# Strided q and k of the first batch: whole 256-byte rows and TensorE transposes in place of half rows and VectorE transposes

## The chip, the cores and the metric

The kernel runs on one core of one Trainium2 chip. The metric is the device time of one execution in microseconds (us); lower is better. The inputs and outputs lie in the chip's memory (HBM), and the kernel is one launch.

## The reference

Three layers, chained. First, attention with 4 batches, 8 heads, 576 tokens and 64 numbers a head. Heads 0 to 3 look at a local window of 32 keys, heads 4 to 7 at the keys of the same residue modulo 32:

```python
rel = pos[:, None] - pos[None, :]
mask_local = (rel >= 0) & (rel < 32)
mask_strided = (rel >= 0) & (pos[None, :] % 32 == pos[:, None] % 32)
scores = np.where(mask, q @ k.T / 8, -1e9)
attn = softmax(scores)                       # + 1e-9 in the denominator
x = (attn @ v) laid out as 2304 tokens x 512
x = (x @ w_a) * (x @ w_b) @ w_out            # 512 -> 1536 -> 512
h = x @ w_in2
out = (h / (1 + exp(-h))) @ w_out2           # 512 -> 2048 -> 512
```

The weights come as 64-bit floats. The kernel rebuilds 32-bit floats from their two halves, and splits each operand into a high and a low part so that three passes of TensorE give the wanted precision.

## The kernel before

The instructions of every engine are written out by hand, in order. Each engine (PE is TensorE, DVE VectorE, ACT ScalarE, POOL GpSimd, SP SyncE's DMA queue) works its own list strictly in that order, and an instruction waits until its inputs are there and its output's place is free.

The start-up, some 55 us, computes the attention of batch 0 alone. It is a loop over stages s from -1 to 16. Units 0 to 4 are the local heads (128 tokens each), units 5 to 8 the strided heads (eight or nine residues each). In stage s the kernel takes scores of unit s, the softmax of unit s-1, the turn (transpose of the probabilities) of unit s-3 and the product with v and the store of unit s-5. Inside a stage the order is the string `ORDER = "AXPV0QWS1LGRTBKUON2Y"`, of which these letters matter here:

- A: at s = 11, 12, 15 and 16 (`PART`) the first half of one up projection of the next layer, into the accumulators acc0 to acc3 in this order (`up(partial[i], ...)`, L683).
- P: TensorE transposes of the local q and k (`turn_pair`, L296) and their copies out of PSUM (L307, L309).
- V and O: the product with v (L540) and the store of x: two copies by ACT (L568), then two subtractions by DVE (L571), all from the PSUM tile of V.
- Q: at s = 2, 3 and 4 (`TQ`) the transposes of the strided q and k (`transpose_qk`, L275).
- S, L, X: the scores (mask L414, product L417), their maximum (L452), the exponential (L466).
- R: at s = 3, 5 and 7 `prepare` copies the strided q of a unit together (L385); it reads all of the transposed q.
- T and U: the turn (L500) and its copy out (L512, L518).
- K: `keep_warm`, products of ones into a bank that nobody reads (L773); `WARM1` says how many in which stage, seven at s = 3.
- 0, B, 1, 2, Y: the conversion of one 64-bit weight piece (L642, L629, L650, L655) and its split (L675, L676), at the stages in `CONV`.

In the first batch every PSUM tile of attention comes from `att_tile`, which deals seven tiles in turn: two "ring", two "att" and acc0, acc1, acc2. The tile that a request gets depends only on how many were asked for before. From s = 15 on it deals four, without the accumulators.

The loads of the start-up are a written list too (`LOADS[-2]`), worked off by SP's queue, a few by ACT's (capital letters). In it t4 and t5 take the strided q and k of batch 0 (`load_qk(1)`, L264): eight transfers, each of 32 partitions x 36 pieces of 128 bytes (half a row of 64 floats), in the layout that DVE's 32x32 block transposes want. Behind them in SP's queue stand the loads of v (L321, L330, L353), weight pieces (L603, L605), and batch 1's q and k (L264 again, the same two buffers).

After the start-up come the blocks of the up and down projections, some 2.7 us of TensorE each, into which the attention of batches 1 to 3 and the conversion of the other weights are planned. The start of the blocks is the end of the start-up; nothing later has a fixed time.

Of the kernel before, what the change touches and what calls it, by code (L numbers as in the profile page):

```python
# [9 lines left out]
F32 = mybir.dt.float32  # L10
# [8 lines left out]
P = 128  # L19
# [14 lines left out]

PREP = {-1: (0, 1, 2, 3, 4), 3: (5, 6), 5: (7,), 7: (8,)}
PAIR = {-1: 0, 0: 1, 2: 2}
TQ = {2: (0,), 3: (1,), 4: (2, 3)}

LOADS = {
    -2: (  # L40
        "q0 Q1 i M1 K2 S1 w0 V1 k0 k1 s1 t4 t5 v0 M7 r8 s1 s1 s1 w2 s2 s1 S1 w1 s1 s1 s1 w4 "
        "w3 s4 Q2 u2 u5 u2"
    ),
    -1: "b",
# [67 lines left out]
def attention_gated_mlp_silu_mlp(  # L112
# [15 lines left out]
    nc = tc.nc  # L128
    B, H, S, D = q.shape
# [32 lines left out]
    lpool = att_ctx.enter_context(tc.tile_pool(name="lpool", bufs=1, side="right"))  # L162
    qpool = att_ctx.enter_context(tc.tile_pool(name="qpool", bufs=2, side="right"))
    apool = att_ctx.enter_context(tc.tile_pool(name="apool", bufs=3, side="right"))

    ident = cpool.tile([P, P], F32, name="ident")
# [11 lines left out]
    def acc_tile(i):  # L178
        return accp.tile([P, 512], F32, tag=f"acc{i}", name=f"acc{i}")

    def ring_tile():
        return ringp.tile([P, 512], F32, tag="ring", name="ring")

    att_turn = [0]
    feed = [nc.sync]

    def att_tile(wide):
        n = att_turn[0]
        att_turn[0] += 1
        if wide:  # L190
            n %= wide
            if n < 2:
                return ring_tile()
            if n >= 4:
                return acc_tile(n - 4)
        return attp.tile([P, 512], F32, tag="att", name="att")
# [19 lines left out]
    def x_tile(g):  # L216
        if g == NG - 1 and g not in x_t:
            both["s"] = t = home(1)
            x_t[g] = two(t[:, :4])
        if g not in x_t:  # L220
            x_t[g] = xpool.tile([P, 2, CC, G], F32R, tag="x%d" % HOMES["x"][g], name="x")
        return x_t[g]
# [10 lines left out]
    class Batch:  # L233
# [38 lines left out]
        def transpose_qk(self, ty, one=None):  # L272
            for i in range(4) if one is None else (one,):
                t, o, c = self.loaded[i // 2], self.T[ty][i // 2], i % 2
                nc.vector.transpose(out=o[:, c], in_=t[:, c].rearrange("p j i -> p (j i)"))  # L275

        def load_pair(self, m, i):

            if not self.T:
                self.T[0] = [qpool.tile([P, 2, S], F32, tag=nm, name=nm) for nm in ("qT", "kT")]  # L280
                self.pairs = {}
            p0, n = PAIRS[m]
            self.pairs[m, i] = t = rpool.tile([P, 4, 2 * D], F32, tag="raw", name="pair")
            feed[0].dma_start(
                out=t[:n],
                in_=(q, k)[i][self.b, 0:4, 2 * p0:2 * (p0 + n), :].rearrange("h (p s) d -> p h (s d)", s=2),
            )
# [345 lines left out]
    def merge_w(c, step, early=False):  # L633
        if c is None or (c < EARLY and not early):
            return
        pair = words[c].rearrange("p (n two) -> p n two", two=2)
        low, high = pair[:, :, 0], pair[:, :, 1]
        if step == 0:
            made[c] = rpool.tile([P, DM], F32, tag="raw", name="raw")
            z = made[c].bitcast(I32)  # L640
            if early:
                nc.vector.tensor_single_scalar(out=z, in_=low, scalar=29, op=ALU.logical_shift_right)  # L642
            else:


                top = words[c].bitcast(U8).rearrange("p (n eight) -> p n eight", eight=8)[:, :, 3]
                nc.scalar.activation(out=z, in_=top, func=AF.Copy, scale=1.0 / 32, bias=-31.0 / 64)  # L647
        elif step == 1:
            z = made[c].bitcast(I32)
            nc.vector.scalar_tensor_tensor(  # L650
                out=z, in0=high, scalar=SIGN, in1=z, op0=ALU.bitwise_and, op1=ALU.bitwise_or
            )
        else:
            z = made[c].bitcast(I32)
            nc.vector.scalar_tensor_tensor(  # L655
                out=z, in0=rebased.pop(c), scalar=3, in1=z, op0=ALU.logical_shift_left, op1=ALU.bitwise_or
            )
            del words[c]
            if c < NA:
                raw[c] = made[c]  # L660
# [19 lines left out]
    def up(ps, w, x, T, chunks=range(CC)):  # L680
        for c in chunks:
            for wi, xi in PASSES:
                nc.tensor.matmul(  # L683
                    ps[:, :T],
                    lhsT=w[:, wi, c * P:(c + 1) * P],
                    rhs=x[:, xi, c, :T],
                    start=(c == 0 and wi == 0 and xi == 0),
                    stop=(c == CC - 1 and wi == 1),
                )
# [73 lines left out]
    with tc.manual_schedule():  # L763
# [6 lines left out]
        def keep_warm(n):  # L770

            for _ in range(n):
                nc.tensor.matmul(idle, lhsT=still, rhs=nc.const_aps.tensor(1.0, [P, 512], BF16), start=True, stop=True)  # L773

        batch = Batch(0, 7)
        nu = len(batch.units)
        every = lambda loads: [None for _ in loads]
        after = Batch(1, False)
        qs0, vs0, q1 = batch.load_qk(1), batch.load_vs(), after.load_qk(0)
        vl0 = batch.load_vl()  # L780

        masks = [epool.tile(list(t.shape), F32, tag="e", name="mask") for t in (mask_loc, mask_str)]
# [32 lines left out]
        for s in range(-1, max(nu + LV, max(PART), max(CONV) + 1) + 1):  # L815
            def stage(f, d):
                if 0 <= s - d < nu:
                    f(s - d)

            if s >= TAIL:  # L820
                batch.wide = 4
            now, last = CONV.get(s), CONV.get(s - 1)
            for step in ORDER:
                if step == "P" and s in PAIR:
                    for i in range(2):
                        batch.turn_pair(PAIR[s], i)
                        batch.turned_pair(PAIR[s], i)
                elif step in "SVTXLGNOU":
                    f, d = {
                        "S": (batch.scores, 0), "L": (batch.largest, 0), "X": (batch.softmax, 1),  # L830
                        "G": (batch.guard, 1), "N": (batch.normalise, 1), "T": (batch.turn, LT),
                        "U": (batch.turned, LT), "V": (batch.values, LV), "O": (batch.store, LV),
                    }[step]
                    stage(f, d)
                elif step == "K":
                    keep_warm(WARM1.get(s, 0))
                elif step == "A" and s in PART:
                    i = PART[s]
                    partial[i] = acc_tile(i)
                    up(partial[i], split[i], x_tile(0), G, (0, 1))  # L840
                elif step == "Q":
                    for i in TQ.get(s, ()):
                        batch.transpose_qk(1, i)
                elif step == "R":
                    for u in PREP.get(s, ()):
                        batch.prepare(u)
                elif step in "012" and now is not None:
                    merge_w(now, int(step), True)
                elif step == "B" and now is not None:
                    rebase_w(now, True)  # L850
                elif step == "Y" and last is not None and last < EARLY:
                    keep_w(last)
                    split_w(last)
                elif step == "W":
                    startup_loads(LOADS.get(s, ""))
        batch = after
# [356 lines left out]
        for m, key in enumerate(in_order):  # L1213
            t = ready[key]
            if m >= 4:
                t = max(t, held[in_order[m - 4]][1])
# [5 lines left out]
        for m, key in enumerate(in_order):  # L1222
            t = used[key][0] - LEAD_SPLIT
            t = max(t, used[in_order[m - 5]][1] if m >= 5 else (m - 5) * BLOCK)
# [34 lines left out]
        for key in in_order:  # L1259
            t = splits[key]  # L1260
# [3 lines left out]
            elif key[0] == "B":  # L1264
                n, c = key[1:]
                kind, j = ("ab"[c], n[1]) if n[0] == "o" else ("i", n[1] + c)
                needs((kind, j), (n, c, 0), t)
            elif key[0] == "B22":
                for c in range(2):
                    n = key[1]  # L1270
                    kind, j = ("ab"[c], n[1] + H1) if n[0] == "o" else ("i", n[1] + c + H2)
                    needs((kind, j), (n, c, 1), t)
            elif key[0] == "T12":
                n, c = key[1:]
# [21 lines left out]
        for m, key in enumerate(in_order):  # L1296
            lo, _, piece = need[key]
            t = lo - LEAD_RAW
            t = max(t, need[in_order[m - 10]][1] + 0.01 if m >= 10 else (m - 10) * BLOCK)
# [3 lines left out]
        p = 0  # L1303
        ys = {}
        for ph, g in PHASES:
# [7 lines left out]
            for kind, j in half[ph]:  # L1313
                if batch.b < B and p == PLAN[batch.b][0]:
                    batch = plan_attention(batch, *PLAN[batch.b])
                work = block(p)
                w = next(work)
                if kind in "abi":
                    rest = range(CC)
                    if p in partial:  # L1320
                        ps, rest = partial[p], (2, 3)
                    else:
                        ps = ring_tile()
# [9 lines left out]
                    else:  # L1333
# [4 lines left out]
                            out=g2, in0=th, scalar=1.0, in1=ps, op0=ALU.add, op1=ALU.mult  # L1338
                        )
                        acts[j] = split_act(g2, T)  # L1340
                elif kind == "o":
                    h = acts.pop(j)
# [9 lines left out]
                    if j == N1 - 1:  # L1352
                        ys[g] = y = xpool.tile([P, 2, CC, G], F32R, tag="x%d" % HOMES["y"][g], name="y")
                        for d in range(CC):
                            nc.scalar.copy(out=y[:, 0, d], in_=accs[d])
                            nc.vector.tensor_tensor(
                                out=y[:, 1, d], in0=accs[d], in1=y[:, 0, d].bitcast(F32), op=ALU.subtract
# [3 lines left out]
                else:  # L1361
                    h = acts.pop(j)
# [14 lines left out]
            for t in range(T // P):  # L1377
                pool, tag = ((epool, "e"), (epool, "e"), (tpool, "a"), (tpool, "h32"))[t]
# [48 lines left out]
```

## Time and profile before

| | us |
|---|---|
| three timed runs | 957.92, 956.31, 957.80 (median 957.80) |
| the profiled execution, its own time | 954.39 |
| its span in the trace | 952.6 |

| engine | busy us | share of the span |
|---|---|---|
| PE | 928.5 | 97% |
| DVE | 663.9 | 70% |
| ACT | 542.6 | 57% |
| POOL | 80.4 | 8% |

The span is the time from the first to the last instruction of the profiled execution; 1.8 us of its own time lie around it. Shares are means over the whole span. The change lies in the first 55 us, so the views below are of that stretch. The mean granted TensorE clock over the span is 0.988 of full speed.

### The profile page before, as it was taken

How to read it: one execution, taken by the hardware profiler on the slowest of the kernel's cores; microseconds unless marked ns; L12 is line 12 of the kernel's file. 1: busy time of each engine (PE TensorE's matmuls, PEld its weight loads, DVE VectorE, ACT ScalarE, POOL GpSimd, SP SyncE). 2: the span in 40 equal slices, each digit the busy share in tenths (PEclk: the TensorE clock that was granted, in tenths of full speed). 3: DMA queues.
4: the chain of work that ended last, by engine and by line, in shares of the span. 5: the costliest groups of instructions: out<-in, count | busy, mean ns of one | idle time of the engine just before them, and what ended most of it. 6: DMA issues, size and time to landing. Idle time of an engine off the chain costs nothing.

```text
span 952.6 us, 15861 instructions
## 1 busy us (share of the span) xinstructions
PE 928.5 (97%) x5626; PEld 749.6 (79%) x5626; DVE 663.9 (70%) x1248; ACT 542.6 (57%) x1274; POOL 80.4 (8%) x138
## 2 busy tenths in 40 slices
PE   9999999999999899999999999999999989999998
PEld 5767777787777677778888888888998768888897
DVE  4588888866767766666777666765587666765475
ACT  3558788566667665465544444345565555554364
POOL 2232222111111110100000000000000000000000
PEclk9799999999999999999999999999999999999999
DMA  9999899898698994322332222223464121234371
GB/s 165 198 271 269 248 254 271 248 294 240 224 267 208 264 223 133 105 86 89 100 105 83 67 67 67 57 83 112 126 185 125 44 67 56 78 107 148 108 212 47
DMA packets 163647, 145.29 MB, mean 153 GB/s; under 512 B 96800, under 2 KB 119904, under 8 KB 163568
## 3 DMA queue, kind: packets, MB, share of 16 engines
q1 hardware_dynamic: 154758, 121.81, 48.1%
q0 software_dynamic: 6720, 21.63, 6.8%
q10 hardware_dynamic: 2090, 0.84, 0.5%
q8 instruction: 44, 0.72, 0.3%
q14 instruction: 35, 0.29, 0.1%
HBM read 121.70 MB, written 22.54 MB: 151 GB/s over the span
## 4 chain that ended last, share of the span: by engine, by line
PE 75%; DVE 11%; ACT 8%; issue 3%; DMA 2%; SPq 0%; DVEq 0%; POOL 0%; ACTq 0%; POOLq 0%
PE ring L683 17%; PE ring L958 10%; PE att L958 8%; PE acc L1019 8%; PE acc L1365 7%; PE acc L1145 4%; PE att L1019 4%; PE ring L1019 4%; PE acc L1345 4%; PE acc L683 3%; ACT prs L466 2%; DVE w L676 2%; DVE raw L650 2%; PE att L540 1%; ACT raw L647 1%
## 5 line engine op out<-in xcount | busy, mean ns | idle before, releaser
L683 PE MATMUL ring<-x,w 128*128 128x512 f32 (+1 forms) x816 | 165.5, 356 | 1.5 <-DVE w L676 1.5
L683 PEld LDWEIGHTS ring<-x,w 128*128 128x128 f32 x816 | 132.4, 189 | 23.4 <-DVE w L676 2.0
L1241 DVE TENSOR_TENSOR w<-raw,w 128x512 fp32r<-128x512 f32 (+1 forms) x164 | 106.3, 656 | 30.3 <-ACT w L1240 27.5
L1240 ACT CAST w<-raw 128x512 fp32r<-128x512 f32 (+1 forms) x164 | 95.8, 593 | 18.6 <-PE att L1019 11.0
L676 DVE TENSOR_TENSOR w<-raw,w 128x512 fp32r<-128x512 f32 x136 | 92.8, 686 | 8.6 <-ACT w L675 7.9
L683 PE MATMUL ring<-y,w 128*128 128x512 f32 x384 | 96.1, 400 | 2.2 <-DVE g L1337 0.8
L1365 PE MATMUL acc<-w,h 128*128 128x512 f32 x384 | 93.9, 394 | 0.0
L683 PEld LDWEIGHTS ring<-y,w 128*128 128x128 f32 x384 | 71.9, 191 | 18.8 <-DVE w L676 1.1
L675 ACT CAST w<-raw 128x512 fp32r<-128x512 f32 x136 | 82.8, 619 | 4.0 <-DVE raw L655 3.9
L1365 PEld LDWEIGHTS acc<-w,h 128*128 128x128 f32 x384 | 70.9, 188 | 15.4
L693 ACT CAST h<-h 128x512 fp32r<-128x512 f32 (+1 forms) x48 | 27.3, 568 | 95.1 <-DVE h L1331 48.1
L1345 PE MATMUL acc<-h,w 128*128 128x512 f32 x288 | 70.8, 395 | 0.0
L958 PE MATMUL ring<-operands,w 128*128 128x512 f32 x240 | 61.4, 398 | 2.4 <-ACT w L1240 2.0
L694 DVE TENSOR_TENSOR h<-g,h 128x512 fp32r<-128x512 f32 (+1 forms) x64 | 39.9, 624 | 33.4 <-ACT h L693 33.2
L1345 PEld LDWEIGHTS acc<-h,w 128*128 128x128 f32 x288 | 53.0, 188 | 11.5
L693 ACT CAST h<-g 128x512 fp32r<-128x512 f32 (+1 forms) x64 | 36.3, 568 | 44.8 <-DVE g L1337 30.4
L958 PE MATMUL att<-operands,w 128*128 128x512 f32 x240 | 60.2, 395 | 0.0
L958 PE MATMUL ring<-x,w 128*128 128x512 f32 x240 | 59.2, 391 | 1.0 <-ACT u L969 1.0
L466 ACT ACTIVATE prs<-sm,nm 128x54 f32<-128x54 f32 (+1 forms) x120 | 39.8, 336 | 30.5 <-DVE nm L452 30.4
L958 PEld LDWEIGHTS ring<-operands,w 128*128 128x128 f32 x240 | 44.7, 188 | 14.8 <-ACT w L1240 2.7
L650 DVE SCALAR_TENSOR_TENSOR raw<-words,raw 128x512 int32<-128x512 int32 x68 | 47.6, 699 | 9.5 <-ACT raw L647 8.9
L958 PEld LDWEIGHTS ring<-x,w 128*128 128x128 f32 x240 | 44.9, 188 | 11.1 <-ACT u L969 1.4
(200 smaller groups left out, 1577.1 us busy)
## 6 DMA issues: line engine op xcount, KB each, us to landing
raw<-keptp SPq DMA_DIRECT2D x80, 256.0 KB
raw<-kepti SPq DMA_DIRECT2D x64, 256.0 KB
words<-in_moe_w_out_dram SPq DMA_DIRECT2D x28, 512.0 KB
raw<-kepto SPq DMA_DIRECT2D x48, 256.0 KB
raw<-kepta SPq DMA_DIRECT2D x36, 256.0 KB
raw<-keptb SPq DMA_DIRECT2D x36, 256.0 KB
words<-in_moe_w_in_dram SPq DMA_DIRECT2D x16, 512.0 KB
words<-in_moe_w_a_dram SPq DMA_DIRECT2D x12, 512.0 KB
```

Of the source, the lines that this page charges most:

```text
L466: nc.scalar.activation(out=place[s], in_=src[:, s], func=AF.Exp, bias=st["nm"][:, s:s + 1], scale=1.0, accum_out=su[:, s:s + 1],)
L650: nc.vector.scalar_tensor_tensor(out=z, in0=high, scalar=SIGN, in1=z, op0=ALU.bitwise_and, op1=ALU.bitwise_or)
L675: nc.scalar.copy(out=o[:, 0], in_=t)
L676: nc.vector.tensor_tensor(out=o[:, 1], in0=t, in1=o[:, 0].bitcast(F32), op=ALU.subtract)
L683: nc.tensor.matmul(ps[:, :T], lhsT=w[:, wi, c * P:(c + 1) * P], rhs=x[:, xi, c, :T], start=(c == 0 and wi == 0 and xi == 0), stop=(c == CC ...
L693: nc.scalar.copy(out=o[:, 0, :T], in_=t32[:, :T])
L958: nc.tensor.matmul(self.acc[acc], lhsT=w[:, wi, (2 * part + c) * P:(2 * part + c + 1) * P], rhs=x[:, xi, c], start=(begin and c == 0 and m ...
L1019: nc.tensor.matmul(accs[d], lhsT=lhsT, rhs=rhs, start=(first and wi == 0 and xi == 0), stop=(last and wi == 1))
L1240: nc.scalar.copy(out=o[:, 0, cols], in_=t)
L1241: nc.vector.tensor_tensor(out=o[:, 1, cols], in0=t, in1=o[:, 0, cols].bitcast(F32), op=ALU.subtract)
L1345: nc.tensor.matmul(accs[d], lhsT=w[:, wi, d * P:(d + 1) * P], rhs=h[:, xi], start=(j == 0 and wi == 0 and xi == 0), stop=(j == N1 - 1 and ...
L1365: nc.tensor.matmul(accs[t][:, :DM], lhsT=h[:, xi, t * P:(t + 1) * P], rhs=w[:, wi, :], start=(j == 0 and wi == 0 and xi == 0), stop=(j == ...
```

## The change

The strided q and k of batch 0 are loaded by `load_rows` instead of `load_qk`: for q and for k, four transfers (one a head) of 128 partitions x 4 rows of 256 bytes for the first 512 tokens, and two transfers of 64 partitions x 2 rows for the last 64. That is 12 transfers instead of 8, and 4608 pieces of 256 bytes instead of 9216 of 128. At step Q, `turn_rows` transposes them on TensorE into a PSUM tile from `att_tile` (four 128x128 transposes for i = 0 to 3, two of 64 tokens for i = 4 and 5) and `turned_rows` copies the tile out, i = 0 and 3 on ACT and the others on DVE. Batches 1 to 3 keep the old way.

```diff
-TQ = {2: (0,), 3: (1,), 4: (2, 3)}
+TQ = {2: (0,), 3: (1, 4), 4: (2, 3, 5)}
+TOKENS = 4
+ROWS_A = (0, 3)
-        "q0 Q1 i M1 K2 S1 w0 V1 k0 k1 s1 t4 t5 v0 M7 r8 s1 s1 s1 w2 s2 s1 S1 w1 s1 s1 s1 w4 "
+        "q0 Q1 i M1 K2 S1 w0 V1 k0 k1 s1 t6 t7 v0 M7 r8 s1 s1 s1 w2 s2 s1 S1 w1 s1 s1 s1 w4 "
+        def load_rows(self, ty):
+            tiles = [lpool.tile([P, TOKENS + 1, 4, D], F32, tag=nm, name=nm) for nm in ("qld", "kld")]
+            self.loaded = tiles
+            self.T[ty] = [qpool.tile([P, 2, S], F32, tag=nm, name=nm) for nm in ("qT", "kT")]
+            whole = P * TOKENS
+            for src, t in zip((q, k), tiles):
+                for h in range(4):
+                    hp, c = divmod(h, 2)
+                    feed[0].dma_start(
+                        out=t[:, :TOKENS, 2 * c + hp],
+                        in_=src[self.b, 4 * ty + h, :whole].rearrange("(n p) d -> p n d", p=P),
+                    )
+                    yield
+                for hp in range(2):
+                    h0 = 4 * ty + 2 * hp
+                    feed[0].dma_start(
+                        out=t[:S - whole, TOKENS, hp::2],
+                        in_=src[self.b, h0:h0 + 2, whole:].rearrange("c p d -> p c d"),
+                    )
+                    yield
+        def turn_rows(self, i):
+            self.turns = getattr(self, "turns", {})
+            self.turns[i] = ps = att_tile(self.wide)
+            if i < 4:
+                parts = [(self.loaded[i // 2][:, n, 2 * (i % 2):2 * (i % 2) + 2], P) for n in range(TOKENS)]
+            else:
+                n = S - P * TOKENS
+                parts = [(self.loaded[i - 4][:n, TOKENS, 2 * c:2 * c + 2], n) for c in range(2)]
+            for m, (t, n) in enumerate(parts):
+                nc.tensor.transpose(ps[:, m * n:(m + 1) * n], t.rearrange("p h d -> p (h d)"), ident[:n, :n])
+        def turned_rows(self, ty, i):
+            ps, o = self.turns.pop(i), self.T[ty][i // 2 if i < 4 else i - 4]
+            copy = nc.scalar.copy if i in ROWS_A else nc.vector.tensor_copy
+            if i < 4:
+                copy(out=o[:, i % 2, :P * TOKENS], in_=ps)
+            else:
+                n = S - P * TOKENS
+                copy(out=o[:, :, P * TOKENS:], in_=ps[:, :2 * n].rearrange("p (c t) -> p c t", c=2))
-        qs0, vs0, q1 = batch.load_qk(1), batch.load_vs(), after.load_qk(0)
+        qs0, vs0, q1 = batch.load_rows(1), batch.load_vs(), after.load_qk(0)
                 elif step == "Q":
                     for i in TQ.get(s, ()):
-                        batch.transpose_qk(1, i)
+                        batch.turn_rows(i)
+                        batch.turned_rows(1, i)
```

## Rows read from the trace of the kernel before

**Rows 1.** The chain of waits, 9 to 54 us: start, length, what held the end.

```profile
9.23 1.06 PE att L296 x8
...
16.42 0.29 PE att L296 x4
...
20.93 0.37 PE att L500 x2
...
47.73 1.40 PE acc L683 x6
...
52.57 0.55 PE acc L773 x2
53.14 0.56 DVE x L571 x2
```

**Rows 2.** Who waited, 9 to 54 us: total us, times, longest.

```profile
DVE nm L452 <- PE ring L417: 4.7, 4, 2.4
...
PE att L296 <- DMA pair<-in_k_dram: 0.5, 1, 0.5
```

**Rows 3.** VectorE's transposes of batch 0: shortest, median, longest in ns.

```profile
L275 DVE STREAM_TRANSPOSE qT<-qld x2: 748/763/778, 17.8 to 19.5; 128x576 f32<-128x576 f32 x2
```

**Rows 4.** Timeline, copies out of PSUM: start, length, engine, line, idle before.

```profile
8.37 0.68 DVE L309 TENSOR_SCALAR qT<-ring 64x512 f32<-64x512 f32 x1 [4.57 <-PE ring L296]
...
60.10 0.58 ACT L1328 COPY a<-acc 128x512 f32<-128x512 f32 x1
```

**Rows 5.** Timeline, VectorE's first transpose and SP's queue around the strided loads.

```profile
8.11 5.60 SPq L264 DMA_DIRECT2D qld<-in_q_dram x4
...
13.76 4.48 SPq L264 DMA_DIRECT2D kld<-in_k_dram x4
...
17.84 0.78 DVE L275 STREAM_TRANSPOSE qT<-qld 128x576 f32<-128x576 f32 x1 [0.16 <-DMA qld<-in_q_dram]
...
27.51 0.40 SPq L605 DMA_DIRECT2D words<-in_moe_w_a_dram  x1
```

**Rows 6.** Timeline of stages 10 and 11: the store of unit 5, its neighbours.

```profile
48.70 0.56 DVE L571 TENSOR_TENSOR x<-acc,x 128x288 fp32r<-128x288 f32 x2
...
50.84 0.42 DVE L518 COPY pt<-ring 118x256 f32<-118x256 f32 x1
```

**Rows 7.** Windows: busy us of each engine, then granted clock, DMA share, GB/s.

```profile
33.00:34.00 1.00, 1.00 (x18) 0.66 (x14) 0.95 (x5) 0.88 (x7) 0.00 (x0) 0.50 1.12 233
...
46.00:47.00 1.00, 1.00 (x23) 0.86 (x24) 0.86 (x4) 1.00 (x3) 0.47 (x2) 0.69 1.33 177
...
60.30:63.72 3.42, 1.22 (x10) 0.59 (x12) 3.42 (x6) 0.38 (x1) 0.00 (x0) 1.00 1.06 219
63.72:67.13 3.41, 3.41 (x36) 2.60 (x36) 2.59 (x7) 2.90 (x8) 0.00 (x0) 0.50 1.01 373
```

**Rows 8.** The chain of waits again, the same work at either clock.

```profile
13.86 0.98 PE acc L773 x4
...
28.98 0.61 PE ring L540 x16
...
31.24 1.25 PE att L417 x12
...
35.91 1.46 PE acc L417 x12
...
37.77 1.71 PE acc L773 x4
39.48 1.05 PE ring L540 x16
...
44.53 0.83 PE acc L500 x3
```

**Rows 9.** DMA of SP's queue (packets, MB, share of 16 engines), 8:18, then 19:27.

```profile
q1 hardware_dynamic: 7068, 1.02, 88.3%
...
q1 hardware_dynamic: 5358, 1.17, 73.2%
```

## Prediction

> **What bounds the kernel now.** The change lies in the start-up, so I read that stretch alone. First the chain of waits from 9 to 54 us [rows 1]. After the last pair of k has landed at 9.23 us, the chain stays on PE, piece after piece, through all stages of the loop until 53.14 us, where it goes over to DVE's subtraction of x (L571). The reader is to see that every piece starts where the one before it ends, and that scores, turns, products with v and fillers all count in it: PE works its list without a pause of its own. Second, who waited in the same stretch [rows 2]: DVE waits for PE's scores, 4.7 us for those in a ring tile alone, and the only DMA wait of PE is 0.5 us, at the start. So in the start-up PE is the bound, DVE and ACT have room, and what lengthens PE's list there moves the beginning of the blocks by as much. Third, the timeline of stages 10 and 11 [rows 6]: there DVE has become dense too, so a pause of PE is not made up behind it. After the start-up nothing is tied to a fixed time, so I pass the delay through to the end one for one.
>
> **What is taken away.** Four VectorE transposes of 0.76 us, 3.1 us in all [rows 3]. They lie on DVE in stages 2 to 4, where DVE sits waiting for PE anyway [rows 2], and PE never waits for one in the chain [rows 1]. Worth nothing on the path; 0 is what I take, and the 0.16 us that the first one waited for its data [rows 5] goes nowhere either.
>
> **What is added on PE.** Sixteen 128x128 transposes and four of 64 tokens, all in stages 2 to 4, in front of the scores of the stage. The nearest rows are the turns, also 128x128 in 32 bits: two in 0.37 us, 0.185 each, with the start of a group in it [rows 1]. The transposes of pairs (128 columns moving, 64 standing) run in eights at 1.06 us, 0.13 each; four of 48 tokens take 0.29 us, 0.07 each [rows 1]. Low end: 16 x 0.13 + 4 x 0.07 = 2.4 us. High end: 16 x 0.185 + 4 x 0.13 = 3.5 us. In groups of four the start weighs half as much as in groups of two, so I take 0.16 and 0.10: 16 x 0.16 + 4 x 0.10 = 3.0 us. No filler is dropped for it, so all of it lengthens the chain.
>
> The page "VectorE: DVE Perf Modes" of the Trainium skill speaks against this change: its section on the three transpose paths gives 390 ns for a 128x128 transpose on TensorE against 311 ns on VectorE, in 16-bit numbers, and its rules call VectorE the fastest for 32x32 blocks. By its figure the sixteen alone would be an estimated 6.2 us. The trace doesn't agree with that as a price in a row, since two turns follow one another in 0.37 us [rows 1], and the sum goes by the trace.
>
> **Copies out of PSUM.** Two of 128x512 on ACT at 0.58 us and two on DVE at 0.68 us, and two of 128x128 on DVE, which I price under half of that [rows 4]. DVE so does some 2 us where it did 3.1; ACT gets 1.2 us, between an exponential and the next maximum, where it waits for DVE and so for PE. The readers of what they write come later in PE's list: q is gathered (L385) after Q in stage 3, and the first strided scores stand at stage 5. Hidden. Without that cover the last ones, i = 2, 3 and 5, would hold the scores of unit 5 by one copy, 0.7 us; I take 0.
>
> **Loads.** SP spends 5.60 + 4.48 = 10.1 us on the eight transfers of 1152 pieces each [rows 5]. A weight transfer of 512 pieces takes it 0.40 us [rows 5]; at that price the new twelve cost at most 4.8 us, though there are four more of them. Everything behind them in SP's queue (v, weights, batch 1's q and k) starts up to 5 us earlier. No engine waits for any of it in the start-up [rows 2], so this is worth 0. The other side: PE now waits for q itself, at the Q of stage 2, behind which stand all of its scores. The trace before has the last q landing at 17.84 us, just when DVE wanted it [rows 5], and PE will want it at about 17.2. If the new q landed no earlier, 0.6 us would be lost; with half as many pieces it lands earlier, and I take 0 of 0 to 0.6.
>
> **What is moved: the PSUM tiles.** This part of the diff has no line of its own. The six new requests to `att_tile` come before stage 5, so every later request gets the tile one place back in the round of seven. Counted through the loop, the product with v of unit 5 (V, stage 10) lands in acc0 where it was in acc1, and the turn of unit 7 in acc1 where it was in acc2. At the very next step A of stage 11 the up projection takes acc0. Before, acc0 had been free since the turn of unit 6, and PE began at 47.73 us [rows 1]. Now PE has to wait until the store of unit 5 has read acc0 to the end: the two DVE subtractions that begin at 48.70 and take 0.56 us, so to 49.26 [rows 6]. That is a pause of 49.26 - 47.73 = 1.5 us, measured in the old times; both sides are shifted alike. Behind the waiting product stand, on PE, V of unit 6 and the turn of unit 8, and for the latter waits DVE's copy at 50.84 us [rows 6], then DVE's whole queue with the splits of the first weights. That copy would come 1.1 us later, and the subtractions of unit 7 the full 1.5. So DVE is what is late next, and almost nothing is absorbed. Bounds 0 (were the store done earlier) and 1.6; I take 1.4. The other accumulators are taken in stages where the last reader is long through, as before.
>
> **Sum.** +3.0 (transposes) + 1.4 (tile) = +4.4 us: the profiled execution's 954.39 would become 958.8. The median of the runs shown is 957.8, 3.4 above the profiled one; on it the forecast is 962.2 us, 0.46% slower.
>
> **The granted clock.** It falls to half (1.2 GHz) at 33 us and is back at full (2.4 GHz) between 46 and 47 [rows 7], in the stretch of strided scores, with PE busy on small products before the fall. The same work stands in either clock [rows 8]: four fillers 0.98 and 1.71 us, sixteen products with v 0.61 and 1.05, twelve strided scores 1.25 and 1.46, a turn 0.185 [rows 1] and 0.28. Six fillers, 40 products with v, 40 scores and seven turns lie in it: 1.1 + 1.1 + 0.7 + 0.6 = 3.5 us that the low clock costs. The transposes come ahead of stage 5, the fall between two groups of strided scores behind it, and the work just before the fall does not change, so I let the clock fall at the same work as before: 0.
>
> **Rivals.**
> 1. The clock holds (not slower). If the added transposes keep TensorE at 2.4 GHz through the strided scores, 3.5 us come back and +0.9 is left: 958.7 us. It decides from about 2.5 us regained, below which the change is still slower. For it: the fall is a matter of what PE did before it, and PE gets 3 us more of work. Against: that work ends before the products in front of the fall begin, and those are the same as before. The Trainium skill, "TensorE: Matmul & The Clock Gate", part 1, says that low clock is the default and activity releases it; that is the mechanism of this rival. The trace agrees as far as its low stretches follow thin work of PE [rows 7].
> 2. The pause at stage 11 is hidden, because the chain there is DVE's already: +3.0, 960.8 us. For it: DVE is dense from 48.7 on [rows 6]. Against: the copy that DVE waits for is a turn behind the pause.
> 3. A second fall of the clock. PE was busy 1.22 of 3.42 us before the low stretch at 63.72 [rows 7]; the pause of 1.5 us might do the same at stages 12 and 13. Then some 2 us of work is done at half speed: +6.4, 964.2 us.
> 4. The start-up or the weights behind it are paced by the transfers (faster). SP's queue moved 7068 pieces in 10 us at 88.3% of 16 engines, 20.0 ns a piece, mostly 128 bytes; later, mostly 256 bytes, 5358 pieces in 8 us at 73.2%, 17.5 ns [rows 9]. So 4608 pieces fewer save 4608 x 20 / 16 = 5.8 us of all engines, and if that were the path, and PE's additions beside it: 952.0 us. Against: PE waits for DMA 0.5 us in the stretch [rows 2].
>
> **How the numbers follow.** Forecast 0.56, rival 1 0.14, rival 2 0.14, rival 3 0.06, rival 4 0.07, and 0.03 that the delay is absorbed later without a name. About 0.2% (1.9 us) is what a measurement of this kernel can tell from no change. Slower: forecast, rivals 2 and 3, 0.76. Rival 1 is mostly within 0.2%, with 0.03 of it faster; with the nameless case that makes 0.14 same, and 0.10 faster. The range: with 2.4 to 3.5 us of transposes, 0 to 1.6 of pause and 0 to 0.6 of waiting for q, the forecast and rivals 2 and 3 lie between 960.2 and 965.5; to take in most of rival 1 it begins at 957.6.
>
> **What would show it.** In the changed profile: twenty transposes in stages 2 to 4 with 2.4 to 3.5 us of the chain; DVE's maxima waiting longer for PE; the strided loads off SP's queue by about 14 us, and vl and vs earlier; at stage 11 a pause of PE in front of the first up projection, released by DVE's L571; the first block's work 4 to 5 us later. Wrong would be: a granted clock of 1.00 through the strided scores, the pause missing, or PE idle at Q for DMA.

## The result and the profile after

| | median us | runs | mean granted clock | ratio to the kernel before, 95% interval |
|---|---|---|---|---|
| changed kernel, first runs | 967.27 | 4 | 0.983 | 1.0103 [1.0069, 1.0137] |
| changed kernel, again | 967.10 | 6 | 0.980 | 1.0130 [1.0092, 1.0168] |
| kernel before, beside the second | 955.34 | 29 | 0.991 | |

The change makes the kernel 1.0 to 1.3% slower, 10 to 12 us. The forecast was 4.4 us and 962.2 us, its range ended at 965.5: the direction was right, the size wrong by more than a factor of two. The profiled execution took 969.26 us, its span 967.5, 14.9 us more than in the kernel before: it is one of the longer ones.

One number of the runs is needed to read all that follows: the mean granted clock of the whole span differs from run to run of one and the same program, and the time goes with it. Of 35 runs of the kernel before that stood beside the first four experiments, those at 0.996 took 951.3 to 954.0 us and those at 0.985 took 959.7 to 960.8.

First the additions that the prediction priced, in the chain of waits of the changed kernel (start, length, what). L313 is the new transposes.

```profile
22.19 1.04 PE ring L313 x4
...
26.90 1.26 PE att L313 x6
...
34.24 0.71 PE acc L313 x4
34.95 0.70 PE ring L313 x6
...
68.45 0.55 DVE x L618 x2
```

All twenty are there, on the chain, but the first ten cost 2.30 us and the last ten 1.41. The subtraction that stood at 53.14 us [rows 1] now stands at 68.45: in this execution the start-up has grown by 15.3 us, not by 4.4, and the whole loss lies in it.

The reason is in the granted clock. Four windows of the changed kernel (busy us of PE, weight loads, DVE, ACT, POOL, then granted clock, DMA share, GB/s):

```profile
12.00:14.00 2.00, 0.30 (x5) 0.21 (x7) 0.14 (x1) 1.99 (x4) 0.16 (x1) 0.99 0.94 172
14.00:34.00 20.00, 19.33 (x173) 12.60 (x176) 5.45 (x22) 7.28 (x38) 1.83 (x3) 0.50 0.75 183
34.00:41.00 7.00, 6.78 (x76) 5.32 (x77) 3.01 (x8) 2.59 (x8) 0.63 (x1) 0.97 0.84 170
41.00:55.00 14.00, 13.73 (x110) 9.64 (x110) 6.58 (x23) 7.87 (x44) 2.46 (x3) 0.51 0.47 100
```

From 14 to 34 us TensorE runs at half clock (1.2 GHz), where the kernel before had it at full until 33 [rows 7]. In the 2 us before the fall PE was busy for 0.30. The fall at the strided scores, which the kernel before has from 33 to 46.6, is there too, from 41 to 55. PE's timeline has the gap, changed kernel:

```profile
11.32 0.55 PE L343 MATMUL ring<-ident,pair 112*64 112x112 f32 x4
13.70 0.27 PE L461 MATMUL ring<-mask_loc,ident_b 128*64 128x256 bf16 x1 [1.82 <-issue]
```

The mask product that opens the scores of unit 0 (L461) writes into the ring tile that ACT's first copy (L354) has to have read: the weight load in front of it waits for ACT's counter, until that copy is done at 13.6 us. ACT was late with it. ACT's timeline, changed kernel (ACTq is a load that ACT itself issues):

```profile
8.82 0.29 ACTq L400 DMA_DIRECT2D vs<-in_v_dram  x1
11.34 0.32 ACTq L331 DMA_DIRECT2D pair<-in_q_dram  x1
11.69 1.28 ACT L354 ACT_TABLE_LOAD   x1 [11.69 <-DMA mask<-in_mask_str_dram]
12.98 0.61 ACT L354 ACTIVATE qT<-ring 64x512 f32<-64x512 f32 x1
```

and the same of the kernel before:

```profile
9.21 0.29 ACTq L353 DMA_DIRECT2D vs<-in_v_dram  x1
9.62 0.32 ACTq L284 DMA_DIRECT2D pair<-in_q_dram  x1
9.97 1.28 ACT L307 ACT_TABLE_LOAD   x1 [9.97 <-DMA pair<-in_k_dram]
11.27 0.62 ACT L307 ACTIVATE qT<-ring 64x512 f32<-64x512 f32 x1
```

ACT's last start-up load, the third pair of q (Q2 of the list), went out at 9.62 us before and at 11.34 after, and everything behind it on ACT came 1.7 us later. (The mask in the bracket is the profile's guess: ACT starts 0.03 us after it has issued that load, and the mask is cast 0.24 us later.) Why the load waited is not in the diff's lines. Every load of SP and ACT is given one of eight completion counters, 0 to 7, in one round over both queues, and may not go out before the last load on its counter has landed; the traces name the counters that each load waits for and reports to. In the kernel before, this load waits for its counter 7 and for counter 0; in the changed kernel for its counter 2 and for counter 0. In the round it stands behind one strided load before the change (counter 4) and behind four after it (4, 7, 0, 1). Counter 2 is that of a load of v issued at 6.13 us, which landed at 11.24; counter 7 was free by 9.3.

Last, stage 11 of the changed kernel, which answers to [rows 6]; the bracket is the idle time before and what ended it:

```profile
62.10 0.56 DVE L618 TENSOR_TENSOR x<-acc,x 128x288 fp32r<-128x288 f32 x2
...
65.67 0.42 DVE L565 COPY pt<-ring 118x256 f32<-118x256 f32 x1 [1.25 <-PE ring L547]
```

```profile
62.80 1.63 PE L730 MATMUL acc<-x,w 128*128 128x512 f32 x6 [2.33 <-DVE x L618]
```

The pause in front of the first up projection is there, released by the store of unit 5 (L618), as predicted, but of 2.33 us where 1.5 was put down. It is not followed by a low clock:

```profile
60.00:70.00 10.00, 7.51 (x87) 5.59 (x89) 7.99 (x19) 5.04 (x16) 8.16 (x11) 1.00 0.76 193
```

### The profile page after: what moved, and what is told of

The parts are those of the page before. It is cut to its first block, busy times and chain, and to the rows that moved or that the text cites. A ratio compares the mean times of both kernels' runs of the same rounds, so it can differ in the third digit from the quotient of the medians.

```text
span 967.5 us, 15906 instructions
## 1 busy us (share of the span) xinstructions
PE 937.4 (97%) x5639; PEld 756.5 (78%) x5646; DVE 662.8 (69%) x1248; ACT 543.4 (56%) x1276; POOL 80.4 (8%) x138
## 4 chain that ended last, share of the span: by engine, by line
PE 75%; DVE 12%; ACT 7%; issue 4%; DMA 2%; ACTq 0%; POOL 0%; DVEq 0%; SPq 0%; POOLq 0%
PE ring L730 18%; PE ring L1006 10%; PE att L1006 8%; PE acc L1067 8%; PE acc L1413 7%; PE acc L1193 4%; PE att L1067 4%; PE ring L1067 4%; PE acc L1393 3%; PE acc L730 3%; ACT prs L513 2%; DVE w L723 2%; DVE raw L697 2%; PE att L587 1%; DVE raw L702 1%
## 5 line engine op out<-in xcount | busy, mean ns | idle before, releaser
L1413 PEld LDWEIGHTS acc<-w,h 128*128 128x128 f32 x384 | 70.9, 188 | 15.3
```

The lines of the kernel that those rows point to most:

```text
L1413: nc.tensor.matmul(accs[t][:, :DM], lhsT=h[:, xi, t * P:(t + 1) * P], rhs=w[:, wi, :], start=(j == 0 and wi == 0 and xi == 0), stop=(j == ...
```

## The experiments

H is the theory just told: ACT's held load, the pause of PE, the fall of the clock. R is the rival that the transposes themselves cost 10 us or pull the clock down. Each ran 12 times beside the kernel before, the changed kernel again six times. They stand in three groups, each on another chip: ACT's list freed, ACT made late, the pause filled and the tile put back; then the changed kernel again, freed with the tile put back, fillers out and the kernel before, freed; then the last four. A ratio is to the kernel before on the same chip, so versions of different groups are compared by their ratios alone.

**The changed kernel again.**

> The changed kernel as it is, once more, for a base of twelve runs beside the experiments of this call: its mean granted clock was 0.983 in four runs against 0.991 of the kernel before. Theory H (ScalarE's held load makes TensorE pause, and the clock falls at 13.8 us in most runs): 963 to 968 us, mean clock 0.980 to 0.986. If the four runs were a chance of the clock: the mean clock of the kernel before, 0.990, and 958 to 960.

967.10 us, mean clock 0.980, as H put down: the first result was no chance of four runs.

**ACT's list freed.** The edit of the changed kernel:

```diff
-  "q0 Q1 i M1 K2 S1 w0 V1 k0 k1 s1 t6 t7 v0 M7 r8 s1 s1 s1 w2 s2 s1 S1 w1 ... w3 s4 Q2 u2 u5 u2"
+  "q0 Q1 i M1 K2 S1 w0 V1 k0 k1 s1 Q2 t6 t7 v0 m7 r8 s1 s1 s1 w2 s2 s1 s1 w1 ... w3 s4 u2 u5 u2"
```

> The changed kernel with ScalarE's last start-up loads rearranged: the third pair of q right behind the two loads of v, the mask and the second piece of v on SP's queue; 12 strided loads, TensorE transposes and the shifted PSUM tiles kept. Theory H (ScalarE is held up by its own load of the third pair until 11.3 us, TensorE pauses 1.8 us at 12 to 13.7, and the granted clock falls to half for the next 20 us): the load goes out by 9.5, the pause is gone, the clock stays at full until the strided scores, and the time is 960 to 963 us. Rival R (the twenty transposes themselves cost 10 us, or pull the clock down): the clock is half through stages 0 to 4 again and the time 966 to 968.

958.75 us, 1.0028 [1.0003, 1.0053], mean clock 0.991 as in the kernel before. Its load went out early, PE did not pause, and the transposes ran at full clock (ACT and PE timeline, then its chain of waits):

```profile
8.85 0.33 ACTq L331 DMA_DIRECT2D pair<-in_q_dram  x1
...
11.22 0.55 PE L343 MATMUL ring<-ident,pair 112*64 112x112 f32 x4
...
11.70 0.30 PE L461 MATMUL ring<-mask_loc,ident_b 128*64 128x256 bf16 x1
```

```profile
16.72 0.59 PE ring L313 x4
19.43 0.70 PE att L313 x6
23.46 0.60 PE acc L313 x4
24.05 0.70 PE ring L313 x6
```

All twenty transposes are there and cost 2.59 us. R is out: the transposes alone make neither the 10 us nor the low clock. The time is below what H put down, by 1 us and more. The list moves the mask to SP's queue too, where it lands late (the run of the kernel before, freed, below); here PE has no pause for it.

**The kernel before, with ACT made late.**

```diff
         startup_loads(LOADS[-2])
+        held = apool.tile([P, 2 * NG_S * JR], F32, tag="sm", name="sm", bufs=1)
+        for _ in range(4):
+            nc.scalar.copy(out=held, in_=nc.const_aps.tensor(1.0, [P, 2 * NG_S * JR], BF16))
```

> The kernel before with four copies of a constant, some 0.4 us each, on ScalarE in front of its first copy out of PSUM: ScalarE is late by 1.7 us as in the changed kernel, and nothing else of the change is there. H: TensorE pauses 1.7 us at 12 to 14, the clock falls there in most runs, and the kernel is slower by 3 to 7 us. R: slower by 0 to 1.8 us, the clock falls at the strided scores as before.

964.19 us, 1.0075 [1.0045, 1.0105], mean clock 0.982. Nothing of the change is in it, and its PE timeline and windows look like those of the changed kernel:

```profile
13.55 0.27 PE L414 MATMUL ring<-mask_loc,ident_b 128*64 128x256 bf16 x1 [1.79 <-issue]
```

```profile
14.00:31.00 17.00, 16.33 (x161) 10.30 (x160) 6.30 (x23) 6.55 (x36) 1.45 (x3) 0.50 0.90 165
31.00:41.00 10.00, 9.85 (x112) 7.29 (x111) 4.80 (x15) 5.62 (x24) 1.68 (x3) 1.00 0.94 212
41.00:58.00 17.00, 16.56 (x129) 12.08 (x129) 10.30 (x27) 8.71 (x43) 5.06 (x6) 0.51 0.58 135
```

So 1.9 us of copies ahead of ACT's first one, at that place, make some 7 us of time (4 to 10 by the interval). Three of the 12 runs stayed under 959 us, so the loss does not come every time.

**The pause filled.** `WARM1` of the changed kernel from `{-1: 2, ...` to `{-1: 10, ...`.

> The changed kernel with ten fillers instead of two at stage -1, eight more of 0.21 us, so that TensorE works where it paused for ScalarE; ScalarE is as late as in the changed kernel. If the granted clock is what makes most of the loss: it stays at full through stages 0 to 4 and the time is 960 to 963 us, though the delay of 1.8 us is still there. If the delay and the transposes make it: 966 to 969 us.

958.23 us, 1.0034 [1.0007, 1.0060], mean clock 0.991. ACT is as late as in the changed kernel (its load at 11.22 us), but PE works in the gap, and the clock stays:

```profile
12.00:14.00 2.00, 2.00 (x19) 1.65 (x17) 1.07 (x2) 1.99 (x4) 0.12 (x1) 1.00 0.98 181
14.00:34.00 20.00, 19.57 (x271) 14.04 (x275) 9.71 (x37) 11.28 (x52) 2.46 (x4) 1.00 0.71 175
```

The time is below both answers, nearer to the first. With the delay and eight fillers more the kernel is at 1.0034, without both (ACT's list freed) at 1.0028, and with the delay and no fillers at 1.0103 to 1.0130. So the delay as such can't be told from nothing on the time, though the first up projection still starts 1.5 us later than in the freed kernel; what costs 7 to 9 us is the clock.

**The PSUM tile put back.** In the changed kernel:

```diff
                         batch.turned_rows(1, i)
+                        att_turn[0] += i == 5
```

> The changed kernel with one more place of the PSUM round skipped after the last transpose, so that every later request has the tile of the kernel before; all else of the change is kept. If the shifted tile costs what the prediction said: faster than the changed kernel by 1.0 to 1.6 us (966 us), and the pause in front of the first up projection at stage 11 is gone. If it is hidden: within 0.5 us of the changed kernel. H and R both: the clock still falls at 13.8.

958.20 us, 1.0044 [1.0008, 1.0080]: neither answer. Seven of its 12 runs lie at 954.4 to 958.4 us with clocks of 0.988 to 0.996, five at 962.9 to 969.3 with 0.978 to 0.987; the profiled one fell at 15 us. Long times came in fewer of its runs than in the changed kernel's, of which nine of ten took more than 962 us, though all that differs comes 10 us and more behind the fall. Six of those ten stood on another chip, which may be the cause and was not tested. The run says nothing of the tile.

**Freed, and the tile put back.** The edit of ACT's list freed and that of the run just told together.

> The kernel of the first experiment (ScalarE's list freed) with the seventh place of the PSUM round skipped as well: of the change only the loads, the transposes and their copies are left. If the shifted tile costs its 1.0 to 1.6 us: 957.2 to 957.8 us, 1.5 above the kernel before. If it is hidden: 958.5 to 959.

956.95 us, 1.0013 [0.9992, 1.0033]: 1.6 us above the kernel before beside it, where without the tile's edit it was 2.7. The intervals overlap, so the times alone don't show what the tile costs; the traces do. On the same chip the changed kernel was at 1.0130, so the two edits together give back some 11 us. The traces of the two can be laid side by side, since they agree within 0.1 us up to 48.4 us. Freed alone, PE, then DVE:

```profile
51.26 1.62 PE L730 MATMUL acc<-x,w 128*128 128x512 f32 x6 [2.33 <-DVE x L618]
```

```profile
54.13 0.42 DVE L565 COPY pt<-ring 118x256 f32<-118x256 f32 x1 [1.25 <-PE ring L547]
...
56.89 0.56 DVE L618 TENSOR_TENSOR x<-ring,x 128x288 fp32r<-128x288 f32 x2 [0.67 <-PE acc L820]
```

and with the tile put back:

```profile
48.77 1.64 PE L730 MATMUL acc<-x,w 128*128 128x512 f32 x6
```

```profile
50.64 0.55 DVE L618 TENSOR_TENSOR x<-acc,x 128x288 fp32r<-128x288 f32 x2
...
52.87 0.42 DVE L565 COPY pt<-ring 118x256 f32<-118x256 f32 x1
...
54.87 0.55 DVE L618 TENSOR_TENSOR x<-att,x 128x288 fp32r<-128x288 f32 x2
```

The pause of 2.3 us is gone, DVE's copy comes 1.3 us earlier and the subtraction of unit 7 2.0 us.

**Fillers out.** `3: 7` to `3: 1` in `WARM1` of the run just told.

> The kernel of the run before with one filler instead of seven at stage 3, where the transposes now give TensorE work: 1.3 us of fillers out for 2.6 us of transposes in. H with the clock held by the transposes as well as by the fillers: 1.3 us less than the run before, 956 to 956.5. If the fillers are what keeps the clock up: it falls earlier, mean clock under 0.988, and 958 to 962.

957.00 us, 1.0019 [1.0002, 1.0037], mean clock 0.990 against 0.992: the 1.3 us did not come, and the clock is a little lower. Between the two answers, so inconclusive.

**The kernel before, freed.** The list of the run with ACT's list freed, with t4 t5.

> The kernel before with ScalarE's list freed in the same way (third pair of q earlier, mask and second piece of v on SP's queue), nothing of the change in it. ScalarE comes some 0.5 us earlier to its first copies, TensorE did not wait for them in the kernel before: 955.5 to 956.2, within 0.1% of it. If ScalarE's list already cost the kernel before something: 1 to 2 us faster.

958.47 us, 1.0043 [1.0018, 1.0067]: a miss on both sides. The moved mask is why. GpSimd's timeline:

```profile
20.88 0.23 POOL L797 CAST mask_str<-mask 128x54 bf16<-128x54 f32 x1 [14.23 <-DMA mask<-in_mask_str_dram]
21.16 1.20 POOL L491 TENSOR_TENSOR prs<-prs,rs 128x256 f32<-128x256 f32 x2
```

On SP's queue the mask lands so late that its cast, and the normalising of units 0 and 1 behind it on GpSimd, wait until 20.9 us. PE's turn (L500) waits for that:

```profile
PE att L500 <- POOL prs L491: 1.4, 1, 1.4
```

The median is 3.1 us longer. Those 1.4 us are not all of it; the mean clock is lower as well, 0.987 against 0.991. The next run tests the mask.

**The kernel before, mended.** The mask stays on ACT, ahead of Q2: `"... k0 k1 s1 M7 Q2 t4 t5 v0 r8 ..."`, the second piece of v on SP.

> The kernel before with ScalarE's list rearranged as in the run before (third pair of q behind the mask, which stays; second piece of v on SP). The loss of 3 us in the earlier run came from the mask, which landed late on SP's queue and held GpSimd's list up to 20.9 us. If that is right: within 0.5 us of the kernel before. If the other moves did it: slower by 2 to 3 us again.

954.68 us, 0.9991 [0.9970, 1.0013]: the loss is gone with the mask back on ACT's queue, so it was the mask. It is no gain that can be told from none. In its profiled run the clock stays at full through the strided scores, where the profiled run of the kernel before had it at half: so the strided scores do not always bring that fall.

**The change, mended.** That list with t6 t7, and the tile put back.

> The changed kernel with both side effects taken out, and the mask left on ScalarE's queue this time: third pair of q behind the mask, second piece of v on SP, seventh PSUM place skipped. Left of the change: loads in whole rows, transposes on TensorE. H: transposes of 2.6 us on the path and no more, 957.5 to 958.5 us if the kernel before stands at 955.5, the clock falling at the strided scores as in the kernel before. If the late mask cost the earlier runs something: 0.5 to 1 us less than that.

956.99 us, 1.0016 [0.9997, 1.0036]: what is left of the change, the loads and the transposes, costs 1.5 us on the ratio, with an interval from -0.3 to 3.4. The 2.6 us of the chain lie inside, and so does nothing. With the mask late the same two edits were at 1.0013, so the late mask cost that run nothing that shows.

**Fillers moved.** In the mended change, `3: 7` to `3: 1`, and `6: 3`, `8: 3` added.

> The mended change with its fillers moved: one instead of seven at stage 3, where the transposes are, and three each at stages 6 and 8, among the strided scores, where the clock falls. The sum of fillers is the same. If the fillers hold the clock there: mean clock 0.994 and more, 953.5 to 955, faster than the kernel before by 1 to 2 us. If the products of ones don't hold it: 957 to 959.

954.79 us, 1.0001 [0.9974, 1.0029], mean clock 0.992: level with the kernel before, but not faster. Ten of its 12 runs lie at 952.0 to 957.8 us, two at 961.7 with a clock of 0.983. That the fillers hold the clock is not shown: from 34 to 44 us it was 0.83 in the profiled run, the same as in that of the mended change with its fillers in the old place. No version is faster than the kernel before beyond the noise.

**Twelve transfers in the kernel before.** Four of the eight strided transfers cut in two, VectorE's transposes kept:

```diff
+                        cs = ((0, 1), (1, 2)) if split and hp < split else ((0, 2),)
+                        for c0, c1 in cs:
...
+                                out=t[p0:p0 + 32, c0:c1].rearrange("r c j i -> r (c j) i"),
...
-        qs0, vs0, q1 = batch.load_qk(1), batch.load_vs(), after.load_qk(0)
+        qs0, vs0, q1 = batch.load_qk(1, 1), batch.load_vs(), after.load_qk(0)
```

> The kernel before with its strided q and k in twelve transfers instead of eight (four of them cut in two, the same pieces of 128 bytes), VectorE's transposes kept. The number of transfers alone moves ScalarE's load of the third pair of q to another of the eight completion counters, that of the second k pair, which in the kernel before is reached at 10.4 us where the load went out at 9.6. H: ScalarE 0.5 to 1 us late, a short pause of TensorE at 12 to 13 us, slower by 0.5 to 3 us with a mean clock below that of the kernel before. R: within 0.5 us of it.

955.67 us, 1.0013 [0.9991, 1.0036]. ACT's and PE's timelines:

```profile
10.49 0.32 ACTq L286 DMA_DIRECT2D pair<-in_q_dram  x1
```

```profile
12.84 0.27 PE L416 MATMUL ring<-mask_loc,ident_b 128*64 128x256 bf16 x1 [0.70 <-POOL mask_str L799]
```

With twelve transfers ACT's load does move, to counter 0 and by 0.9 us, to the 10.4 us at which the second pair of k lands, and PE pauses for it, 0.70 us. (The bracket names GpSimd's cast of the mask; ACT's first copy, done at 12.75 us, is what came last.) But the clock holds there in the profiled run, and the time shows nothing, as R had it. So the first half of H is shown, the lateness and the pause, and the price here is nil. The changed kernel has twelve transfers too, but counter 2: in the round the load stands there behind four strided loads and here behind two. The number of transfers alone does not give the changed kernel's counter; what sets the order of the round was not tested.

## Why the prediction was wrong

1. **Loads: the step that failed.** "No engine waits for any of it in the start-up [rows 2], so this is worth 0." I followed the new transfers through SP's queue alone. ACT issues loads too, in its one list with its copies, and the new transfers came ahead of its last load in the round of counters, which moved it to a counter that came free 1.7 us later. The list of waits of the kernel before, from 9 to 54 us, had the sign, and I read past it:

```profile
ACT L307 <- DMA pair<-in_k_dram: 10.0, 1, 10.0
```

ACT did nothing before 9.97 us but issue loads. Its first copy ran from 11.27 to 11.89 us, and PE wrote into the tile behind it from 12.20: 0.3 us of room, where the prediction had "DVE and ACT have room". PE stood still for 1.82 us once the copy came 1.7 us later.

2. **The granted clock: the size.** "... so I let the clock fall at the same work as before: 0." It is 7 to 9 of the 10 to 12 us. Rival 1 had the clock hold at the strided scores; rival 3 had the right mechanism, a pause of PE and a low clock behind it, but for the pause at stage 11, and priced at 2 us. That pause came and the clock stayed at 1.00; the fall came at 14.0 us, behind a pause that no rival had. The Trainium skill, "TensorE: Matmul & The Clock Gate", part 1, has an active TensorE released to the full clock. In the changed kernel the profile counts PE busy for 19.33 of 20 us at half clock, so the busy share of the profile's page doesn't show what the clock will be.

That the kernel got slower, as forecast, is in good part luck: some 2.7 of the 10 to 12 us come from terms that the sum had.

3. **Transposes: right.** 3.0 us were put down, 2.4 to 3.5 as bounds; 2.59 us at full clock. In the changed kernel they cost 3.71 because half of them ran at half clock. Four in a row take 0.59 us, 0.15 each. The Trainium skill, "VectorE: DVE Perf Modes", the three transpose paths, gives 390 ns for one on TensorE in 16-bit numbers. That is not the price in a row here.

4. **Copies, VectorE's transposes: right.** Nothing of them is on the chain.

5. **The shifted PSUM tile: the mechanism right, the size too small.** The pause was to be 1.5 us and was 2.33, over the bound of 1.6. The copy behind it was to come 1.1 us later and came 1.3 later, the subtraction 1.5 and came 2.0. That "both sides are shifted alike" failed: with the tile put back, PE begins the up projection at 48.77 us and the store ends at 51.19, 2.4 us apart where the old times gave 1.5. On the time, 1.4 us were put down; the two runs differ by 1.1, within their noise.

6. **SP's queue itself: worth nothing, as put down, but its price was wrong.** The twelve transfers took it 8.5 us instead of 10.1, where "at most 4.8" was put down, since it waits for counters between them, and it was through with them at 16.5 us, not "about 14":

```profile
7.71 3.59 SPq L290 DMA_DIRECT2D qld<-in_q_dram  x4
11.51 1.40 SPq L297 DMA_DIRECT2D qld<-in_q_dram  x2
12.95 2.25 SPq L290 DMA_DIRECT2D kld<-in_k_dram  x4
15.24 1.26 SPq L297 DMA_DIRECT2D kld<-in_k_dram  x2
```

Without the held load, the two priced terms gave 2.7 us (ACT's list freed; 0.3 to 5.1 by its interval) where 4.4 were forecast.

## What to carry to other kernels

When a change adds loads, follow every load behind them on every queue, also those that a compute engine issues in its own list: if completion counters are dealt in turn, more loads ahead of one change which counter it waits for. Count what a pool deals in turn the same way: six more PSUM requests moved a tile that was wanted ten stages later. Where TensorE runs small products, price a new pause by the clock that may follow it, not by its length alone, and look at more than three runs.

## What the runs showed that was not expected

A pause of TensorE of 1.8 us at about 12 us was followed by 17 to 20 us at half clock (the kernel before with ACT late; the changed kernel), with PE busy almost all of that time. The length of the pause does not decide alone: 0.70 us at the same place was not followed by half clock, and neither was 1.4 us at 20.5 us (the kernel before, freed), nor 2.33 us in front of the first up projection (the changed kernel), in the runs that were profiled. A wait of PE for the second pair of k at 8 to 9 us, 1.01 us in the changed kernel and 0.47 in the kernel before, does not explain it: the profiled run of the moved fillers has 0.95 there and its clock holds until 37 us, and that of the changed kernel with the PSUM tile put back has 0.32 there and its clock falls at 15. What decides stays open.

The kernel before has mean clocks of 0.983 to 0.998 over the 99 runs beside the experiments, and 951 to 961 us with them. Why nine of ten runs of the changed kernel took more than 962 us, and only five of 12 with the PSUM tile put back, stays open.
